# Off-by-one softmax attention and a mish MLP on one core: five tiles transposed wholly by DMA, copies, loads and outputs put in another order

## The chip, the core and the metric

One core of a Trainium2 chip runs the whole kernel. Its engines work side by side: TensorE (PE: matmuls, with the weight loads as PEld), VectorE (DVE), ScalarE (ACT), GpSimd (POOL) and SyncE (SP, which here only issues DMAs). Each runs its own list of instructions in order, and they wait for one another through semaphores. Data moves between HBM and the on-chip memory (SBUF) by DMA. In this kernel SP's queue carries all loads of q, k and v, all DMA transposes and nearly all stores; POOL's queue carries the weights. Matmul results land in PSUM, in banks of 512 fp32 numbers per partition.

The metric is the device time of one execution, in microseconds. The profile covers one execution; its times count from the start of its span.

## The reference

```python
# q, k, v: (8, 12, 448, 64) float32; moe_w_in: (768, 2048); moe_w_out: (2048, 768)
scores = matmul(q, k^T) / sqrt(64)
m = max(scores, axis=-1)
e = exp(scores - m)
attn = e / (sum(e, axis=-1) + exp(-m) + 1e-09)
x = matmul(attn, v), heads put side by side           # (3584, 768)
h = x @ moe_w_in
out = (h * tanh(softplus(h))) @ moe_w_out             # mish, then the second matmul
```

## The kernel before

*Pairs, units, stages.* The 12 heads of a batch are taken two at a time: 48 pairs, 6 in a batch. Three pairs make a unit. The first six pairs (0 to 5, the head) run by themselves in the loop at L663; from pair 6 on, the loop at L698 takes one unit after the other: unit 2 is pairs 6 to 8, unit 3 pairs 9 to 11, unit 4 pairs 12 to 14 and so on. In each unit the attention of its three pairs (12 steps) runs beside work of earlier pairs, and then comes half a batch of the first MLP matmul with its mish (the loop at L795). From unit 4 on, the second MLP matmul of earlier batches is spread over the 12 steps as filler for TensorE. Units 2 and 3 have no such filler. The head has matmuls on a constant (`keep_busy`, L287) in its place.

*One pair.* q, k and v come as fp32 (`load_pair`, L133) and are cast to bf16, mostly by POOL (`cast`, L177). q and k are transposed, by TensorE into PSUM (`transpose_pair`, L207) for pairs up to 17 and by DMA (`turn_by_dma`, L197) from 18 on. `evac_qk` (L238) copies the transposed q, scaled, and k to SBUF: one of VectorE, ScalarE or POOL. In the head, ScalarE takes both copies of the even pairs (`act=True`, L674; pair 1 too, L667) and VectorE those of the odd ones.

A pair has four steps of scores (`scores`, L309), each into one of three PSUM tiles `sc` of two banks. The fourth step fills one bank only. VectorE takes the negated row maximum (L350), ScalarE the exp with the row sum (`exps`, L355, L366), into the tile `en`. `scores_ahead` (L302) keeps three steps in flight, so a unit's first four scores are issued at its very start.

*The transposed probabilities.* `normalise` (L428) divides where that is done early and starts the DMA transpose of `en` into `eT` (L440): four chunks of 112 keys, seven blocks of 128x128 each. For pairs 0 to 4 the DMA takes three chunks, and TensorE the fourth (`turn_on_pe`, L445, with seven transposes and a copy by VectorE, L455). For pairs 5, 6 and 7 (`BY_PE`, L640) TensorE turns all of it. There are three `eT` buffers, so the transposes of pairs 3 and 4 wait until the outputs of pairs 0 and 1 have read theirs.

*The outputs.* `av_pair` (L463) multiplies `eT` by v, eight matmuls, three pairs later, and a copy takes the result into `xT`, input of the MLP. In the head and at the end the result goes to a bank of its own. In units 2 and 3 it goes into the second bank of a pair's fourth score tile, which is free (`half`, L469). From unit 4 on `scores` itself calls it, ahead of the fourth step's score, into that same bank (L323). A unit's first pair of outputs needs the `eT` that the unit before issued last among its work; for unit 5 that is pair 12.

*The weights.* `load_w` (L165) issues the next n of 20 pieces on POOL's queue: 12 of `moe_w_in`, 8 of `moe_w_out`. With `behind`, POOL first copies two elements of a pair's `eT`, so that it waits for that transpose to land. Before: 6 behind pair 4 (L687), 2 in unit 2 (L645), 5 behind pair 8 (L799), 3 in unit 3, 4 behind pair 10 (L801).

*The loads.* SP issues in the order of the program, and each load waits for a buffer (three of each kind). In units 2 to 4, steps 0, 3 and 6 (`LOAD_AT`, L636) load q and k of the pair four ahead and v of the next, and cast what came before (L735 to L740).

Of the kernel before, what the change touches and what calls it, by code (L numbers as in the profile page):

```python
# [15 lines left out]
UNIT_PAIRS = 3  # L16
# [3 lines left out]
def kernel(  # L20
# [288 lines left out]
    def scores(idx):  # L309
# [13 lines left out]
        if s == STEPS - 1 and p in av_with:  # L323
            av_pair(av_with.pop(p), bank=sc[:, 1, :], beside=idx)
# [28 lines left out]
        st["sc", s] = (sc, cols)  # L353

# [73 lines left out]
    def normalise(p, dma=True):  # L428
        st = att[p]
        en = st["en"]  # L430
        for i in range(NTILE if divided(p) else 0):
            nc.vector.tensor_scalar(  # L432
                out=en[:, :, i, 0:SP_], in0=en[:, :, i, 0:SP_],
                scalar1=st["rden"][:, i : i + 1], scalar2=None, op0=ALU.mult,
            )
        eT = eT_pool.tile([128, NT, 2 * S], BF16, tag="eT", name="eT")
        st["eT"] = eT
        if dma:
            n = NT - 1 if p < HEAD else NT
            nc.sync.dma_start_transpose(  # L440
                out=eT[:, 0:n, :].rearrange("c j (i q) -> c (j i) q", q=128),
                in_=en[:, 0:n].rearrange("q j i c -> q (j i c)"),
            )
# [19 lines left out]
    def av_pair(p, bank=None, beside=None, half=None, hold=False):  # L463
# [5 lines left out]
        if half is not None:  # L469
            bank = free_half(half)  # L470
            mms = av_beside.setdefault(half * STEPS + STEPS - 1, [])
        av = mo_take() if bank is None else bank
# [17 lines left out]
        def evac():  # L490
            to = xT[b][:, hp, :]
            if divided(p):
                read = (nc.scalar.copy if p in BY_PE else nc.vector.tensor_copy)(out=to, in_=av[:, 0:S])  # L493
# [4 lines left out]
            if half in half_exp:  # L498
                apart(read, half_exp[half])
            elif beside is not None or half is not None:  # L500
                av_read[beside if half is None else half * STEPS + STEPS - 1] = read
            if bank is None:
# [142 lines left out]
    W_AT = ({5: 2}, {1: 3})  # L645
# [17 lines left out]
    for p in range(HEAD):  # L663
        for s in range(STEPS):
# [8 lines left out]
            if s == 2:  # L673
                evac_qk(p + 2, act=p % 2 == 0)  # L674
# [5 lines left out]
            if s == 1 and p:  # L680
                turn_on_pe(p - 1, NT - 1)
            if s == 2:
# [3 lines left out]
                if p == HEAD - 1:  # L686
                    load_w(6, behind=p - 1)  # L687
# [10 lines left out]
    for u in range(UNITS_PER_B, N_UNITS + 2 * UNITS_PER_B):  # L698
# [11 lines left out]
        for n in range(steps):  # L710
# [24 lines left out]
            if n in LOAD_AT and u <= first_mm2:  # L735
                at = p0 + LOAD_AT.index(n)
                load_pair(at + LEAD, "qk")
                load_pair(at + 1, "v")
                cast(at + LEAD - 1, "qk")
                cast(at, "v")  # L740
# [54 lines left out]
        for f in range(FF_U):  # L795
            if moe:
                mm1_mish(b, w * FF_U + f)
            if u == UNITS_PER_B and f == 3:
                load_w(5, behind=p0 + 2)  # L799
# [52 lines left out]
```

## Time and profile before

| | us |
|---|---|
| median of three runs | 466.2 (465.72 to 466.34) |
| the profiled execution | 465.11 |
| its span, first to last instruction | 463.3 |
| TensorE busy | 441.6 (95%) |
| VectorE busy | 347.3 (75%) |
| ScalarE busy | 331.9 (72%) |
| POOL busy | 184.6 (40%) |

The median of the runs is 1.1 us above the profiled execution, and that one is 1.8 above its span. The granted TensorE clock was 0.991 on average, and full except in the first 20 us and the last.

A row of the timeline gives start, length, engine (SPq and POOLq are the queues' own), line, operation, output and inputs, the count of merged instructions, and in brackets how long the engine idled before and what ended that. A row of groups gives the busy time and mean ns of one after the bar, then the idle time before the group. A row by stage gives the stretch, its length, the busy time of each engine with instruction counts, the granted clock, the DMA share (the 16 engines' mean busy share; it passes 1 where packets of two queues overlap) and GB/s. In what follows "tile p" is the `eT` of pair p.

### The profile page before, as it was taken

How to read it: one execution, taken by the hardware profiler on the slowest of the kernel's cores; microseconds unless marked ns; L12 is line 12 of the kernel's file. 1: busy time of each engine (PE TensorE's matmuls, PEld its weight loads, DVE VectorE, ACT ScalarE, POOL GpSimd, SP SyncE). 2: the span in 40 equal slices, each digit the busy share in tenths (PEclk: the TensorE clock that was granted, in tenths of full speed). 3: DMA queues.
4: the chain of work that ended last, by engine and by line, in shares of the span. 5: the costliest groups of instructions: out<-in, count | busy, mean ns of one | idle time of the engine just before them, and what ended most of it. 6: DMA issues, size and time to landing. Idle time of an engine off the chain costs nothing.

```text
span 463.3 us, 8712 instructions
## 1 busy us (share of the span) xinstructions
PE 441.6 (95%) x2975; PEld 242.8 (52%) x2975; DVE 347.3 (75%) x674; ACT 331.9 (72%) x876; POOL 184.6 (40%) x267
## 2 busy tenths in 40 slices
PE   6878998999999999999999999999999999999996
PEld 3334555445555555555555555555555554556563
DVE  5899879688798998989898979889888969311021
ACT  4999888798797878787887978787878778221300
POOL 4434629043256271736464643727363610100000
PEclk8899999999999999999999999999999999999999
DMA  8999999999999999999999999999999492911122
GB/s 237 252 209 234 223 225 208 220 233 248 234 268 268 230 253 215 293 223 269 235 270 244 270 219 242 255 234 241 260 271 238 118 253 59 253 48 35 34 69 68
DMA packets 232492, 97.93 MB, mean 211 GB/s; under 512 B 189312, under 2 KB 228992, under 8 KB 232448
## 3 DMA queue, kind: packets, MB, share of 16 engines
q1 hardware_dynamic: 224928, 91.06, 83.0%
q0 software_dynamic: 7488, 6.29, 8.7%
q8 instruction: 23, 0.38, 0.3%
q14 instruction: 21, 0.17, 0.1%
q10 hardware_dynamic: 32, 0.02, 0.0%
HBM read 45.61 MB, written 11.01 MB: 122 GB/s over the span
## 4 chain that ended last, share of the span: by engine, by line
PE 70%; ACT 12%; DVE 10%; DMA 4%; issue 2%; SPq 0%; DVEq 0%; ACTq 0%
PE mo L532 26%; PE mo L595 23%; ACT en L366 10%; PE sc L329 7%; DVE negm L350 7%; PE sc L480 6%; PE sc L532 4%; DMA eT<-en 2%; DMA q_f<-in_q_dram 1%; DVE xT L493 1%; DVE eT L455 1%; PE sc L335 1%; DMA k_f<-in_k_dram 1%; PE mo L480 1%; DVE o_sb L578 1%
## 5 line engine op out<-in xcount | busy, mean ns | idle before, releaser
L366 ACT ACTIVATE en<-sc,negm 128x448 bf16<-128x448 f32 x336 | 209.4, 642 | 29.5 <-DVE negm L350 27.7
L350 DVE TENSOR_REDUCE negm<-sc 128x2 f32<-128x896 f32 x192 | 180.9, 969 | 42.3 <-PE sc L329 33.1
L595 PE MATMUL mo<-w_out_sb,gT 128*128 128x384 bf16 (+1 forms) x1024 | 166.7, 306 | 0.4 <-DVE rb L420 0.4
L532 PE MATMUL mo<-xT,w_in_sb 128*128 128x448 bf16 x660 | 132.2, 352 | 1.5 <-ACT gT L548 0.9
L595 PEld LDWEIGHTS <-gT 128*128 128x128 bf16 x1024 | 96.4, 98 | 56.1 <-issue 1.9
L270 POOL TENSOR_SCALAR qd<-qT_all 64x448 bf16<-64x448 bf16 x60 | 80.1, 1335 | 85.5 <-DMA qT_all<-q_cast 65.0
L532 PEld LDWEIGHTS <-w_in_sb 128*128 128x128 bf16 x768 | 74.2, 98 | 70.4 <-issue 4.1
L548 ACT ACTIVATE gT<-mo 128x448 bf16<-128x448 f32 x110 | 58.3, 544 | 68.0 <-PE mo L532 67.9
L432 DVE TENSOR_SCALAR en<-en,rden 128x448 bf16<-128x448 bf16 x280 | 89.2, 394 | 0.6
L366 ACT ACTIVATION_READ_ACCUMULATOR en<-sc,negm 128x1 f32 x336 | 71.6, 213 | 0.0
L578 DVE COPY o_sb<-mo 128x384 f32<-128x384 f32 (+1 forms) x64 | 31.9, 498 | 50.1 <-PE mo L595 49.3
L329 PE MATMUL sc<-kT_all,qd 128*128 128x448 bf16 x252 | 67.6, 354 | 0.0
L480 PE MATMUL sc<-eT,v_bf 112*64 112x448 bf16 x336 | 39.8, 357 | 2.0 <-ACT en L366 1.1
L329 PEld LDWEIGHTS <-qd 128*128 128x128 bf16 x252 | 24.6, 98 | 28.7 <-issue 12.9
L191 POOL CAST q_cast<-q_f 112x512 bf16<-112x512 f32 x47 | 28.7, 611 | 5.2 <-DMA q_f<-in_q_dram 5.2
L480 PEld LDWEIGHTS <-v_bf 112*64 112x64 bf16 x384 | 19.9, 109 | 20.5 <-issue 12.9
L742 POOL COPY marks<-en 1x2 bf16<-1x2 bf16 x12 | 2.1, 174 | 68.6 <-DVE en L432 68.6
L191 POOL CAST k_cast<-k_f 112x512 bf16<-112x512 f32 x47 | 28.6, 609 | 0.8 <-PE sc L329 0.5
L191 POOL CAST v_bf<-v_f 112x512 bf16<-112x512 f32 x48 | 28.1, 607 | 1.7 <-DMA v_f<-in_v_dram 1.7
L532 PE MATMUL sc<-xT,w_in_sb 128*128 128x448 bf16 x108 | 23.2, 353 | 0.0
L493 DVE CAST xT<-sc 128x448 bf16<-128x448 f32 x35 | 21.5, 615 | 0.0
L548 ACT ACT_TABLE_LOAD x14 | 18.0, 1283 | 0.8 <-PE mo L532 0.2
(64 smaller groups left out, 235.3 us busy)
## 6 DMA issues: line engine op xcount, KB each, us to landing
k_f<-in_k_dram SPq DMA_DIRECT2D x48, 224.0 KB, 5.1
q_f<-in_q_dram SPq DMA_DIRECT2D x48, 224.0 KB, 4.9
v_f<-in_v_dram SPq DMA_DIRECT2D x48, 224.0 KB, 5.0
w_in_sb<-in_moe_w_in_dram POOLq DMA_DIRECT2D x12, 256.0 KB, 8.9
w_out_sb<-in_moe_w_out_dram POOLq DMA_DIRECT2D x8, 384.0 KB, 12.2
out_dram<-o_sb SPq DMA_DIRECT2D x7, 336.0 KB, 3.5
out_dram<-o_sb SPq DMA_DIRECT2D x8, 288.0 KB, 4.8
out_dram<-o_sb SPq DMA_DIRECT2D x8, 240.0 KB, 3.8
```

The costliest lines, as they stand in the source:

```text
L191: nc.gpsimd.tensor_copy(out=to[nm], in_=src)
L270: q_reads.append(by.tensor_scalar(out=qd[rows, :, h, :], in0=q_ps[rows, 0:S].rearrange("d (i r) -> d i r", i=QB), scalar1=SCALE, scalar2=N ...
L329: nc.tensor.matmul(sc[:, bk, 0:S], lhsT=qT[:, i].rearrange("d h r -> d (h r)"), rhs=kT, start=True, stop=True,)
L350: half_max[p] = nc.vector.tensor_reduce(out=negm, in_=sc[:, 0 : len(cols), 0:S], axis=AX.X, op=ALU.max, negate=True)
L366: e = nc.scalar.activation(out=st["en"][:, :, c, 0:SP_], in_=sc[:, bk, 0:S].rearrange("q (j c) -> q j c", j=NT), func=AF.Exp, bias=st["neg ...
L432: nc.vector.tensor_scalar(out=en[:, :, i, 0:SP_], in0=en[:, :, i, 0:SP_], scalar1=st["rden"][:, i : i + 1], scalar2=None, op0=ALU.mult,)
L480: mm = nc.tensor.matmul(av[h * 64 : (h + 1) * 64, 0:S], lhsT=v_bf[:, h, j * D : (j + 1) * D], rhs=e_h, start=(j == 0), stop=(j == NT - 1),)
L493: read = (nc.scalar.copy if p in BY_PE else nc.vector.tensor_copy)(out=to, in_=av[:, 0:S])
L532: nc.tensor.matmul(bank[:, 0:S], lhsT=w_in_sb[:, dm, ff * 128 : (ff + 1) * 128], rhs=xT[b][:, dm, :], start=(dm == 0), stop=(dm == DM_T - 1),)
L548: nc.scalar.activation(out=gT[:, ff, b % 2 * S : b % 2 * S + S], in_=h_ps[:, 0:S], func=AF.Mish)
L578: nc.vector.tensor_copy(out=o_sb[:, cols.start : cols.start + n_dve], in_=st["o"][:, 0:n_dve])
L595: nc.tensor.matmul(st["o"][:, 0:n_cols], lhsT=gT[:, ff, i * 128 : (i + 1) * 128], rhs=w_out_sb[:, ff, cols], start=(ff == 0), stop=(ff == ...
```

## The change

- Pairs 0 to 4: all four chunks of `eT` by DMA. `turn_on_pe` is no longer called for them.
- In the head, VectorE makes the copies of q and k of every pair from 2 on.
- Weights: 3 pieces behind tile 3, 3 behind tile 4, none in the steps of unit 2, 7 behind tile 8; the other seven as before.
- Loads: v of pair 8 comes first in unit 2; v of 7, q and k of 12 and v of 9 move from the steps of unit 2 into its MLP loop, behind the transpose of tile 8. The cast of v of 7 moves to the start of unit 3.
- Outputs from unit 4 on: called behind the fourth step's score and its maximum, with the bookkeeping that units 2 and 3 use (`half`). The copy of pair 7's output moves from ScalarE to VectorE; pair 6's stays.

```diff
@@ scores
-        if s == STEPS - 1 and p in av_with:
-            av_pair(av_with.pop(p), bank=sc[:, 1, :], beside=idx)
...
         st["sc", s] = (sc, cols)
+        if s == STEPS - 1 and p in av_with:
+            av_pair(av_with.pop(p), half=p)
@@ normalise
-            n = NT - 1 if p < HEAD else NT
             nc.sync.dma_start_transpose(
-                out=eT[:, 0:n, :].rearrange("c j (i q) -> c (j i) q", q=128),
-                in_=en[:, 0:n].rearrange("q j i c -> q (j i c)"),
+                out=eT.rearrange("c j (i q) -> c (j i) q", q=128),
+                in_=en.rearrange("q j i c -> q (j i c)"),
             )
@@ av_pair
-        av = mo_take() if bank is None else bank
+        av = mo_take() if half is None else free_half(half)
...
-                read = (nc.scalar.copy if p in BY_PE else nc.vector.tensor_copy)(out=to, in_=av[:, 0:S])
+                by_act = p == HP
+                read = (nc.scalar.copy if by_act else nc.vector.tensor_copy)(out=to, in_=av[:, 0:S])
+                if by_act:
+                    apart(read, half_max[half])
@@ head loop
-                evac_qk(p + 2, act=p % 2 == 0)
+                evac_qk(p + 2)
...
-            if s == 1 and p:
-                turn_on_pe(p - 1, NT - 1)
...
-                if p == HEAD - 1:
-                    load_w(6, behind=p - 1)
+                if p >= HEAD - 2:
+                    load_w(3, behind=p - 1)
@@ weights in steps
-    W_AT = ({5: 2}, {1: 3})
+    W_AT = ({}, {1: 3})
@@ unit loop, steps
-                load_pair(at + LEAD, "qk")
-                load_pair(at + 1, "v")
+                if u > UNITS_PER_B or n < LOAD_AT[-1]:
+                    load_pair(at + LEAD, "qk")
+                if u > UNITS_PER_B:
+                    load_pair(at + 1, "v")
+                elif n == 0:
+                    load_pair(at + 2, "v")
+                if u == UNITS_PER_B + 1 and n == 0:
+                    cast(at - 2, "v")
                 cast(at + LEAD - 1, "qk")
-                cast(at, "v")
+                if u > UNITS_PER_B or n != LOAD_AT[1]:
+                    cast(at, "v")
@@ unit loop, MLP
+            if u == UNITS_PER_B and f == 2:
+                load_pair(p0 + 1, "v")
+                load_pair(nxt + UNIT_PAIRS, "qk")
+                load_pair(nxt, "v")
             if u == UNITS_PER_B and f == 3:
-                load_w(5, behind=p0 + 2)
+                load_w(7, behind=p0 + 2)
```

9 lines of the change are left out of this document (4 added, 5 removed).

## The prediction

> **What bounds the kernel now.** I read the page's shares, then the busy time by stage, then the chain of waits, then the timeline of the queues. Stages (start:end, then length and busy time of each engine, granted clock, DMA share):
>
> ```profile
> core 0: us, PE busy (x) PEld busy (x) DVE busy (x) ACT busy (x) POOL busy (x), PEclk, DMA share, GB/s
> 13.77:39.43 25.66, 20.14 (x187) 10.12 (x187) 23.35 (x40) 24.88 (x83) 7.77 (x21) 0.99 1.13 223
> 92.40:118.50 26.10, 24.66 (x183) 13.81 (x181) 20.61 (x41) 21.59 (x56) 9.22 (x16) 1.00 1.13 237
> 118.50:144.26 25.76, 25.39 (x158) 13.84 (x157) 23.42 (x49) 20.38 (x53) 12.03 (x14) 1.00 1.11 259
> 144.26:169.60 25.34, 25.24 (x159) 13.89 (x158) 22.13 (x43) 20.27 (x53) 13.18 (x16) 1.00 1.05 243
> ```
>
> Three regimes stand here. In the head (pairs 1 to 5) ScalarE is busy 24.88 of 25.66 us, VectorE 23.35; TensorE waits for them, and part of its 20.14 is filler. In the units behind it TensorE is busy 25.24 of 25.34 us. And everywhere the DMA share is over 1: the 16 engines always have something queued. Between head and steady state the chain goes through that queue. The chain's piece, and TensorE's row at its end:
>
> ```profile
> 112.32 10.99 DMA eT<-en
> ```
> ```profile
> 123.44 0.95 PE L480 MATMUL sc<-eT,v_bf 112*64 112x448 bf16 x8 [0.37 <-DMA eT<-en]
> ```
>
> The page's median from issue to landing, for the same transfer:
>
> ```profile
> eT<-en SPq DMA_TRANSPOSE x45, 5.4
> ```
>
> The first tile of the unit that ends at 118 (pair 12) takes 10.99 us where 5.4 is usual, as it stands in its queue behind loads and shares the engines with weights; TensorE then waits 0.37 us. So at 123.3 TensorE and DMA arrive together. Whatever the head gains passes into the total only if that tile also lands earlier.
>
> **The change part by part.** *Transposes.* Five tiles go from 21 blocks of 128x128 to 28; 35 transposes on TensorE and five VectorE copies vanish. SP's queue (start, time to issue):
>
> ```profile
> 13.98 3.68 SPq L440 DMA_TRANSPOSE eT<-en  x1
> ...
> 25.99 3.65 SPq L440 DMA_TRANSPOSE eT<-en  x1
> ...
> 30.35 0.41 SPq L140 DMA_DIRECT2D k_f<-in_k_dram  x1
> 31.52 3.28 SPq L440 DMA_TRANSPOSE eT<-en  x1
> ...
> 35.52 0.41 SPq L140 DMA_DIRECT2D k_f<-in_k_dram  x1
> 37.30 3.28 SPq L440 DMA_TRANSPOSE eT<-en  x1
> ...
> 57.85 5.71 SPq L440 DMA_TRANSPOSE eT<-en  x1
> ...
> 85.56 11.38 SPq L440 DMA_TRANSPOSE eT<-en  x3
> ...
> 112.32 15.61 SPq L440 DMA_TRANSPOSE eT<-en  x3
> ```
>
> Three full tiles in an emptied queue take 11.38, that is 3.79 each; tiles of three chunks 3.28. Marginal cost 0.5 a tile, 2.5 us for five. Bounds: by blocks 3.79 x 7/28 = 0.95 a tile, 4.7 us; from below 0.14 (3.79 against 3.65), 0.7 us. I take 2.5, as the 3.28 rows are the ones with an undisturbed issue. Against it stands queue time that is free now: SP has nothing to issue from 30.76 to 31.52 and from 35.93 to 37.30 (2.1 us), since tiles 3 and 4 wait for a buffer that the outputs of pairs 0 and 1 release, and these come earlier when the head is faster.
>
> By the Trainium skill (VectorE: DVE Perf Modes, "The three transpose paths" and "Rules for kernel authors"), a 128x128 transpose costs 390 ns on TensorE and 1309 ns by DMA, with TensorE recommended; 35 moved blocks would then add 45.8 us of DMA time against 13.7 saved. The rows above disagree: a full tile of 28 blocks is issued in 3.79 us. By them the rule's warning shrinks to the range given.
>
> *ScalarE and VectorE in the head.* Groups of that stage (count, busy us, mean ns), then ScalarE's and VectorE's timeline:
>
> ```profile
> L455 DVE COPY eT<-mo 112x896 bf16<-112x896 bf16 x4 | 2.5, 615 | 0.0
> ...
> L261 ACT ACTIVATE qd<-mo 128x448 bf16<-128x448 bf16 x2 | 1.1, 554 | 0.0
> L280 ACT COPY kT_all<-mo 128x448 bf16<-128x448 bf16 x2 | 1.1, 552 | 0.0
> ```
> ```profile
> 13.77 0.28 ACT L379 ACTIVATE expm<-negm 128x7 f32<-128x7 f32 x1
> ...
> 20.28 0.63 ACT L366 ACTIVATE en<-sc,negm 128x448 bf16<-128x448 f32 x1 [0.60 <-DVE negm L350]
> ...
> 22.73 0.55 ACT L261 ACTIVATE qd<-mo 128x448 bf16<-128x448 bf16 x1
> ...
> 23.57 0.68 ACT L366 ACTIVATE en<-sc,negm 128x448 bf16<-128x448 f32 x1
> ...
> 39.43 0.22 ACT L379 ACTIVATE expm<-negm 128x7 f32<-128x7 f32 x1
> ```
> ```profile
> 18.04 0.61 DVE L455 COPY eT<-mo 112x896 bf16<-112x896 bf16 x1
> 18.57 0.38 DVE L263 TENSOR_SCALAR qd<-mo 128x448 bf16<-128x448 bf16 x1
> ...
> 19.17 2.61 DVE L350 TENSOR_REDUCE negm<-sc 128x2 f32<-128x896 f32 x3
> ```
>
> The two ScalarE copies hold the chain of exps from 22.73 to 23.57, 0.84 us. They leave for pairs 2, 4 and 6: 2.5 us of the engine that sets this stage. VectorE takes the same two for 0.60 (18.57 to 19.17), 1.8 us in all, and loses five copies of 0.53 (18.04 to 18.57), 2.7 us; so it carries 0.9 less, but in every pair now, close to ScalarE's load. I take 2.0 us off the head; bounds 0 (VectorE's reductions end last instead) and 3.0 (ScalarE's 0.60 us of waiting at 20.28, where one pair has the transposed copy and the q and k copies on VectorE, goes too). The TensorE transposes sat beside filler, and cost nothing before or after.
>
> *Weights and loads.* POOL's queue:
>
> ```profile
> 42.71 0.17 POOL L169 COPY marks<-eT 1x2 bf16<-1x2 bf16 x1 [2.42 <-DMA eT<-en]
> 42.83 4.54 POOL L174 DMA_DIRECT2D w_in_sb<-in_moe_w_in_dram  x6
> ...
> 51.16 1.46 POOL L174 DMA_DIRECT2D w_in_sb<-in_moe_w_in_dram  x2
> ...
> 67.20 0.17 POOL L169 COPY marks<-eT 1x2 bf16<-1x2 bf16 x1 [8.20 <-DMA eT<-en]
> ```
>
> Three pieces leave some 6 us sooner, behind tile 3 (31.52 + 5.4 = 36.9, against 42.71); two pieces (51.16) and four loads go behind tile 8, whose 5.71 us of issue (57.85) shows a full queue in front of it. The number of pieces and loads ahead of tile 12 stays the same, so these edits only reorder work of a queue that is never empty: 0. The new mark makes POOL wait, with the scale factors and the casts of pair 8 queued behind it; those are used only in the next unit. Cover gone, the three issues (4.54 / 2 = 2.3 us) would show. From the other side: if the queue runs dry in front of tile 8 because four loads now stand behind it, the dry time is lost, up to the 5.71 - 3.79 = 1.9 us that the backlog cost there.
>
> *Outputs behind scores.* Steady units, TensorE, VectorE, ScalarE:
>
> ```profile
> 152.91 0.81 PE L595 MATMUL mo<-w_out_sb,gT 128*128 128x384 bf16 x4
> 153.67 0.95 PE L480 MATMUL sc<-eT,v_bf 112*64 112x448 bf16 x8
> ...
> 157.84 0.66 PE L595 MATMUL mo<-w_out_sb,gT 128*128 128x192 bf16 x6
> 158.60 0.95 PE L480 MATMUL sc<-eT,v_bf 112*64 112x448 bf16 x8
> ```
> ```profile
> 150.09 0.62 DVE L350 TENSOR_REDUCE negm<-sc 128x1 f32<-128x448 f32 x1 [1.27 <-PE sc L329]
> ```
> ```profile
> 150.75 0.63 ACT L366 ACTIVATE en<-sc,negm 128x448 bf16<-128x448 f32 x1 [0.63 <-DVE negm L350]
> ```
>
> Today the fourth score of a pair stands behind eight output matmuls (0.95 us); VectorE idles 1.27 and ScalarE 0.63 for it. Swapped, both get it 0.9 us sooner. TensorE itself loses little to it: normally the outputs start 0.05 us before the previous row's modelled end (153.67 against 153.72), in every second unit 0.10 behind it (158.60 against 158.50), so 0.15 us a unit pair; six pairs give 0.9 us. Bounds 0 (the same wait moves to the score) and 1.8 (twice that). Waiting outputs no longer hold a score. The moved copy of pair 7's output costs VectorE one such row,
>
> ```profile
> L493 DVE CAST xT<-sc 128x448 bf16<-128x448 f32 x35 | 21.5, 615 | 0.0
> ```
>
> 0.6 us, in a stretch whose end waits for DMA anyway.
>
> **Sum.** Tile 12's landing: +2.5 (blocks) - 2.1 (queue time now unused) - 0.7 (the first tile is issued at 13.98, right behind pair 0's last exps at 13.77, and one 0.84 leaves before that; most of it counts) = -0.3. The head's 2.0 does not pass beyond this, and turns into a longer wait at tile 12. Steady units: -0.9. Together -1.2 us. The profiled execution took 465.11 (span 463.3 and 1.8 around it), so 463.9; the three runs' median is 466.2, 1.1 above it, so 465.0. Bounds: landing -2.8 (2.1 and 1.4 of an earlier start against 0.7) to +4.7, steady 0 to -1.8.
>
> **The rivals.**
> - *The gain passes whole.* If tile 12 is no longer late, the total keeps the head's 2.0 and the units' 0.9: 463.3; with the head at 3.0, 462.3. For it: the first three tiles show that loads behind them keep the engines full, so a seventh more blocks may fit. Against: DMA shares of 1.13 in both stages.
> - *The extra blocks are paid in full (slower).* Blocks cost 0.95 a tile, nothing is absorbed, tile 12 lands 4.7 us later, at 128.0, and TensorE waits there. With 0.9 back from the units that is +3.8: 470.0. It decides as soon as the landing slips by more than 0.9. For it: tile 12's 10.99 us, and 15.61 for its three tiles against 11.38. Against: 3.28 for three chunks and 3.79 for four.
> - *The head isn't shortened.* VectorE's copies in each pair delay its reductions by the 0.60 that ScalarE gets back, and tiles are issued no earlier: +2.5 at the landing, -0.9: 467.8.
> - The Trainium skill (DMA: Bandwidth & Descriptors, "Queues, rings and completion order") says that each DMA engine takes turns between queues packet by packet, so weights issued earlier would slow tile 4 and speed nothing; that is the second rival's mechanism, and no row of this profile separates it.
>
> **How the numbers follow.** Forecast 0.40 (own range 463.5 to 466.5), gain whole 0.10, paid in full or most of it 0.30, head not shortened 0.20. Within 0.2% (0.93 us, about what a measurement of this kernel can tell from no change) lie a quarter of the forecast's chance (0.10) and, where the third rival is half absorbed, 0.10 of it: same 0.20. Faster 0.30 + 0.10 = 0.40. Slower 0.40. The range takes the head's 3.0 at the low end and all blocks paid at the high end, each cut a little: 462.5 to 469.5.
>
> **What would show it.** Right: ScalarE's two copies gone from the head and the expm row of pair 5 near 37.4 instead of 39.43; full tiles there issued in about 3.8 us; tile 12 landing near 123 and a TensorE wait in front of its outputs of about 2 us instead of 0.37; units of about 25.2 us. Wrong: tile 12 landing at 125 or later (blocks paid), no wait for it at all (gain passes), POOL or TensorE waiting for weights or for casts of pairs 8 and 12, or a VectorE busier than 95% of the head. The forecast falls if any unit behind 120 grows longer than 25.34.

## The result, and the profile after

The kernel after takes 472.94 us (median of six runs, 472.2 to 475.0), the kernel before 465.99 beside it (465.68 to 467.78). The ratio is 1.0146, 95% interval 1.0119 to 1.0173: 7 us slower, outside the range of the prediction and on its other side. Here and below, medians are over all runs and ratios over the undisturbed ones alone, so that the two can differ by some tenths of a per cent.

The profiled execution of after is the slowest of its six (475.0, span 473.2, mean granted clock 0.978), so its trace holds 9.9 us more than that of before, not 7. Where they arise is read off the row in which ScalarE loads its table for the mish of each MLP, one row a unit:

| start of the MLP of | before | after | difference |
|---|---|---|---|
| unit 2 | 57.84 | 59.37 | +1.5 |
| unit 3 | 85.56 | 85.57 | 0.0 |
| unit 4 | 109.88 | 116.11 | +6.2 |
| unit 5 | 136.68 | 146.33 | +9.7 |
| the last | 389.89 | 400.15 | +10.3 |

So nearly all of it (9.7 of 10.3 us) is lost before 147 us, in units 2, 4 and 5, and unit 3 wins 1.5 back. The busy time by stage of after, with the columns as before:

```profile
12.22:37.29 25.07, 21.10 (x166) 8.97 (x166) 24.11 (x43) 23.48 (x79) 8.53 (x21) 0.93 1.14 233
93.40:125.30 31.90, 26.47 (x183) 14.30 (x182) 20.99 (x42) 21.62 (x57) 9.29 (x16) 0.95 1.17 225
125.30:154.70 29.40, 27.01 (x159) 14.28 (x158) 22.95 (x50) 20.42 (x54) 13.25 (x17) 0.94 1.05 255
154.70:180.10 25.40, 25.33 (x159) 13.60 (x158) 21.73 (x43) 20.15 (x54) 13.28 (x18) 1.00 0.99 235
```

The head ends 2.1 us earlier, where 2.0 was forecast (expm of pair 5):

```profile
37.29 0.25 ACT L379 ACTIVATE expm<-negm 128x7 f32<-128x7 f32 x1
```

One pair of executions fixes this only roughly: in the traces of before, after and the kernels below this row starts at 39.4 to 41.1 us where the head is that of before (four traces, mean 40.1), and at 36.9 to 37.7 where it is that of after (six, mean 37.2). VectorE is busy 24.11 of the 25.07 us, 96%.

Units 4 and 5, which took 26.10 and 25.76 us, take 31.90 and 29.40. TensorE is idle in them for the difference between length and busy time, 5.4 and 2.4 us, and the clock of 0.95 and 0.94 makes its busy time longer too. Behind them a unit takes 25.40, where it took 25.34. SP's transposes and POOL's queue up to that point:

```profile
12.67 5.51 SPq L439 DMA_TRANSPOSE eT<-en  x1
...
19.90 6.69 SPq L439 DMA_TRANSPOSE eT<-en  x1
...
27.81 4.50 SPq L439 DMA_TRANSPOSE eT<-en  x1
...
33.54 4.05 SPq L439 DMA_TRANSPOSE eT<-en  x1
...
38.83 4.56 SPq L439 DMA_TRANSPOSE eT<-en  x1
...
59.38 3.56 SPq L439 DMA_TRANSPOSE eT<-en  x1
...
85.57 17.69 SPq L439 DMA_TRANSPOSE eT<-en  x3
```
```profile
41.30 0.18 POOL L169 COPY marks<-eT 1x2 bf16<-1x2 bf16 x1 [8.58 <-DMA eT<-en]
41.42 2.38 POOL L174 DMA_DIRECT2D w_in_sb<-in_moe_w_in_dram  x3
...
47.96 0.18 POOL L169 COPY marks<-eT 1x2 bf16<-1x2 bf16 x1 [2.55 <-DMA eT<-en]
48.08 2.17 POOL L174 DMA_DIRECT2D w_in_sb<-in_moe_w_in_dram  x3
50.25 0.21 POOL L391 CAST hl<-rden 128x7 bf16<-128x7 f32 x1
```

The five tiles of the head take 25.31 us to issue (5.51 + 6.69 + 4.50 + 4.05 + 4.56). In before they take 19.28: the four rows that the prediction shows, and tile 1, which it left out:

```profile
19.38 5.39 SPq L440 DMA_TRANSPOSE eT<-en  x1
```

That is 6.0 more for 35 blocks, 1.2 a tile, where 0.5 was taken and 0.95 was the bound. The mark rows date two landings: tile 3 at 41.3, tile 4 at 47.96, 5.2 us later than the 42.71 of before, although it was issued only 1.5 us later (38.83 against 37.30). POOL then issues three pieces, and only behind them come the scale factors of pair 5, at 50.25. In before:

```profile
47.33 0.25 POOL L391 CAST hl<-rden 128x7 bf16<-128x7 f32 x1
```
```profile
51.25 0.70 PE L411 MATMUL mo<-ident,hl 128*64 128x128 bf16 x16
```

There they were begun at 47.33 and used at 51.25, 3.9 us later. With the shorter head TensorE wants them 3 us sooner, and they come 2.9 us later. TensorE's three rows with a long wait in after, all of it new except the first 0.37 us of the last:

```profile
50.51 1.27 PE L411 MATMUL mo<-ident,hl 128*64 128x128 bf16 x16 [2.40 <-POOL hl L391]
...
101.26 1.71 PE L478 MATMUL sc<-eT,v_bf 112*64 112x448 bf16 x8 [4.85 <-DMA eT<-en]
...
131.65 1.54 PE L478 MATMUL sc<-eT,v_bf 112*64 112x448 bf16 x8 [2.39 <-DMA eT<-en]
```

They wait for the factors of pair 5, for tile 9 and for tile 12 (which landed at 131.6 instead of 123.3). What makes each worse stands in the length of the row: the same sixteen or eight matmuls take 0.70 and 0.95 us in other places, and 1.27, 1.71 and 1.54 here. Three stretches of unit 2 in after, by stage:

```profile
50.00:53.00 3.00, 2.49 (x24) 1.37 (x24) 0.00 (x0) 1.12 (x4) 2.91 (x8) 0.50 1.15 303
53.00:57.00 4.00, 4.00 (x16) 1.18 (x13) 2.54 (x3) 2.00 (x7) 1.24 (x3) 0.53 0.99 169
...
58.00:60.50 2.50, 2.50 (x19) 1.15 (x16) 2.09 (x6) 2.48 (x6) 0.48 (x3) 1.00 0.00 0
```

Behind the wait the granted clock (third column from the right) is 0.50 and stays there for some 6.8 us. And from 58.0 to 60.5 the DMA share is 0.00: the queue that "is never empty" is empty, since the loads that stood there wait behind tile 8. It was not always full in before either: between 122 and 123 us, right ahead of tile 12's landing at 123.3, the DMA share is 0.11, and in after it is 0.14 between 130 and 131, ahead of the landing at 131.6. So the last microsecond before that landing is not a wait behind other bytes; what it is, no run here shows.

### The profile page after: what moved, and what is told of

It is laid out like the page before. It is cut to its first block, busy times and chain, and to the rows that moved or that the text cites. A ratio compares the mean times of both kernels' runs of the same rounds, so it can differ in the third digit from the quotient of the medians.

```text
span 473.2 us, 8561 instructions
## 1 busy us (share of the span) xinstructions
PE 447.2 (95%) x2940; PEld 241.0 (51%) x2940; DVE 349.7 (74%) x676; ACT 328.5 (69%) x869; POOL 185.5 (39%) x268
## 4 chain that ended last, share of the span: by engine, by line
PE 78%; DMA 6%; DVE 5%; ACT 5%; issue 4%; POOL 2%; SPq 1%; DVEq 0%; POOLq 0%
PE mo L596 27%; PE mo L533 26%; PE sc L327 9%; PE sc L478 8%; PE sc L533 4%; ACT en L366 4%; DMA eT<-en 4%; DVE negm L348 4%; DMA k_f<-in_k_dram 1%; POOL w_in_sb L174 1%; PE sc L333 1%; PE sc L290 1%; PE sc L225 1%; PE mo L478 1%; SPq L140 1%
## 5 line engine op out<-in xcount | busy, mean ns | idle before, releaser
L596 PE MATMUL mo<-w_out_sb,gT 128*128 128x384 bf16 (+1 forms) x1024 | 168.4, 308 | 0.0
L596 PEld LDWEIGHTS <-gT 128*128 128x128 bf16 x1024 | 93.8, 98 | 66.9 <-issue 16.5
L270 POOL TENSOR_SCALAR qd<-qT_all 64x448 bf16<-64x448 bf16 x60 | 80.0, 1334 | 89.5 <-DMA qT_all<-q_cast 39.2
L478 PE MATMUL sc<-eT,v_bf 112*64 112x448 bf16 x336 | 41.9, 373 | 7.2 <-DMA eT<-en 7.2
L478 PEld LDWEIGHTS <-v_bf 112*64 112x64 bf16 x384 | 18.7, 111 | 32.0 <-issue 22.6
L748 POOL COPY marks<-en 1x2 bf16<-1x2 bf16 x12 | 2.1, 176 | 67.4 <-DVE en L432 67.4
```

The lines of the kernel that those rows point to most:

```text
L270: q_reads.append(by.tensor_scalar(out=qd[rows, :, h, :], in0=q_ps[rows, 0:S].rearrange("d (i r) -> d i r", i=QB), scalar1=SCALE, scalar2=N ...
L478: mm = nc.tensor.matmul(av[h * 64 : (h + 1) * 64, 0:S], lhsT=v_bf[:, h, j * D : (j + 1) * D], rhs=e_h, start=(j == 0), stop=(j == NT - 1),)
L596: nc.tensor.matmul(st["o"][:, 0:n_cols], lhsT=gT[:, ff, i * 128 : (i + 1) * 128], rhs=w_out_sb[:, ff, cols], start=(ff == 0), stop=(ff == ...
```

## The experiments

All are variants of the kernel before or of the kernel after; each ran beside the kernel before on the same chip.

### One part of the change at a time

*Outputs behind scores, alone.*

```diff
-        if s == STEPS - 1 and p in av_with:
-            av_pair(av_with.pop(p), bank=sc[:, 1, :], beside=idx)
...
         st["sc", s] = (sc, cols)
+        if s == STEPS - 1 and p in av_with:
+            av_pair(av_with.pop(p), half=p)
```

> The kernel before with one edit: from unit 4 on the outputs stand behind the fourth score. Queue theory (the loss is made by the DMA queue: tiles 9 and 12 land late): nothing is changed in the queue, so 466.0 within 0.8 us, units of the steady state 25.3 to 25.4 us. Order theory (outputs behind scores hold up TensorE): most of the 7 us, 470 or more. The prediction on record had 0.9 us of gain for this edit, 465.1.

466.84 us, ratio 1.0012 (0.9984 to 1.0041): nothing that can be measured. The wait is not removed; it has another name. In its trace the second pair of a unit now holds ScalarE up:

```profile
154.37 0.64 ACT L366 ACTIVATE en<-sc,negm 128x448 bf16<-128x448 f32 x1 [1.51 <-DVE negm L348]
```

With a wait of 0.40 later in this unit that makes 1.91 us; in the same unit of before ScalarE waited 0.63, 0.81 and 0.51, or 1.95.

*Five tiles wholly by DMA, alone.*

```diff
-            n = NT - 1 if p < HEAD else NT
+            n = NT
...
-            if s == 1 and p:
-                turn_on_pe(p - 1, NT - 1)
```

> The kernel before with one edit: pairs 0 to 4 turned wholly by DMA, no fourth chunk on TensorE. Queue theory: seven blocks cost 0.7 to 0.95 us of queue time a tile, 3.5 to 4.7 us, and tile 12 lands near 127 in place of 123.3: 468.5 to 471. Prediction on record: 0.5 us a tile, and no more than 466.8. Rival (the queue had room; the loss is in the moved weights and loads): 466 within 0.8.

472.18 us (four runs), ratio 1.0119 (1.0087 to 1.0152): 5.5 us, most of the loss. POOL, then TensorE, in its trace:

```profile
46.93 0.18 POOL L169 COPY marks<-eT 1x2 bf16<-1x2 bf16 x1 [7.86 <-DMA eT<-en]
47.05 4.52 POOL L174 DMA_DIRECT2D w_in_sb<-in_moe_w_in_dram  x6
51.57 0.21 POOL L391 CAST hl<-rden 128x7 bf16<-128x7 f32 x1
```
```profile
51.83 0.93 PE L411 MATMUL mo<-ident,hl 128*64 128x128 bf16 x16 [2.03 <-POOL hl L391]
...
55.00 0.93 PE L532 MATMUL mo<-xT,w_in_sb 128*128 128x448 bf16 x2 [0.87 <-DMA w_in_sb<-in_moe_w_in_dram]
...
57.26 0.93 PE L532 MATMUL mo<-xT,w_in_sb 128*128 128x448 bf16 x2 [1.33 <-DMA w_in_sb<-in_moe_w_in_dram]
```

Tile 4 lands 4.2 us later than in before, and everything that hangs behind it is late at once: the factors (2.03 us of waiting), then the first weights (0.87 and 1.33). Unit 2's MLP begins at 62.5 instead of 57.8, and these 4.7 us stay, the larger part of the 6.9 at the last MLP (396.8 against 389.9). A wait of 1.65 us for tile 15 in unit 6 adds most of the rest. There is no wait at tile 12 in this one: the price is paid in unit 2, not where the prediction looked.

*VectorE's copies of q and k, alone.*

```diff
-                evac_qk(p + 2, act=p % 2 == 0)
+                evac_qk(p + 2)
```

> The kernel before with one edit: VectorE makes the q and k copies of all pairs from 2 on in the head, and keeps the five copies of the fourth chunk. Queue theory: whatever the head gains or loses up to 2 us is swallowed at tile 12, 465.5 to 466.5. Rival (VectorE's load in the head is what costs): pair 5's last exps later than 39.4 and 467.5 or more.

465.40 us, ratio 0.9984 (0.9955 to 1.0014): no change. The head itself is not shorter. Its expm of pair 5 starts at 39.92, within the 39.4 to 41.1 us of the unchanged head, and VectorE is now the busiest engine of that stage (here in the stretch of before's):

```profile
13.77:39.43 25.66, 21.10 (x184) 10.12 (x183) 24.69 (x46) 23.07 (x75) 8.27 (x22) 0.94 1.09 231
```

24.69 of 25.66 us, and 26.36 of 27.50, 96%, in this kernel's own stage (12.42 to 39.92). Where three or all five of the PSUM copies of the fourth chunks go as well, this row stands at 36.9 to 38.1; where they go and ScalarE keeps its copies of q and k, at 39.2 and 38.6. The head's gain takes both edits.

*The kernel after, fourth chunk back on TensorE.*

```diff
-                out=eT.rearrange("c j (i q) -> c (j i) q", q=128),
-                in_=en.rearrange("q j i c -> q (j i c)"),
+                out=eT[:, 0 : (NT - 1 if p < HEAD else NT), :].rearrange("c j (i q) -> c (j i) q", q=128),
+                in_=en[:, 0 : (NT - 1 if p < HEAD else NT)].rearrange("q j i c -> q (j i c)"),
...
+            if s == 1 and p:
+                turn_on_pe(p - 1, NT - 1)
```

> The changed kernel with one part undone: the fourth chunk of pairs 0 to 4 on TensorE again, with VectorE's copy. Queue theory: the queue loses 3.5 to 4.7 us of blocks, tiles 9 and 12 land that much sooner than in the changed kernel, and POOL's wait for tile 4 shrinks: 467.5 to 469.5. Rival (the reordered weights and loads, or the order of outputs, make the loss): 472 or more, as the changed kernel.

470.15 us, ratio 1.0072 (1.0047 to 1.0097): still 3.4 us slower than before, with not one block more on the DMA queue. The outputs and the copies of q and k cost nothing alone, nor does pair 7's copy (below), so this is left for the reorder of weights and loads. The two prices, 5.5 and 3.4, add up to more than the 7 us of the whole change; they are in part the same lateness. How the reorder costs, its queues tell (SP, POOL, TensorE), though the profiled execution is far the slowest of its eight (475.57 us, the next 471.15), so that its waits are longer than usual:

```profile
36.86 9.17 SPq L439 DMA_TRANSPOSE eT<-en  x1
```
```profile
35.59 2.40 POOL L174 DMA_DIRECT2D w_in_sb<-in_moe_w_in_dram  x3
...
51.94 0.17 POOL L169 COPY marks<-eT 1x2 bf16<-1x2 bf16 x1 [12.09 <-DMA eT<-en]
```
```profile
54.50 0.93 PE L411 MATMUL mo<-ident,hl 128*64 128x128 bf16 x16 [3.62 <-POOL hl L391]
```

Tile 4, of three chunks as in before, is issued 0.4 us earlier than there and lands 9.2 us later, at 51.94. The three pieces of weights behind tile 3 were put on POOL's queue just ahead of it.

### What the reorder costs, and where

*Factors first on POOL.* In the kernel after:

```diff
-                if p >= HEAD - 2:
+                if p == HEAD - 2:
                     load_w(3, behind=p - 1)
...
     denominators(HEAD - 1)
+    load_w(3, behind=HEAD - 2)
```

> The kernel after, with one change: the three weights behind tile 4, and the mark that makes POOL wait for that tile, stand behind the scale factors of pair 5 in POOL's queue instead of in front of them. Theory (POOL's queue): TensorE's wait of 2.40 us for these factors at 50.51 is gone, the granted clock stays at 1.0 there (it was 0.50 from 52 to 56), unit 2's MLP starts near 55.5 instead of 59.4, and tile 8 is issued as much earlier; if that passes through, about 469. Rival (the DMA queue sets the end): tiles 9 and 12 land when they did (101.3, 131.6), TensorE waits the longer for them, and the time stays within 1 us of 472.9.

469.95 us, ratio 1.0065 (1.0034 to 1.0096): 3.0 us back. The wait for factors is gone, the clock is 1.00 through unit 2, whose MLP begins at 55.6, as the theory had it. Tile 9 still lands late, and TensorE waits there as long as in after (4.90 us, with the clock at 0.50 behind it), since it arrives sooner. The wait at tile 12 has gone. The number lies between the two theories: a part passes, a part turns into waiting.

*Loads back.* In the kernel after, the four loads return to unit 2's steps:

```diff
-                if u > UNITS_PER_B or n < LOAD_AT[-1]:
-                    load_pair(at + LEAD, "qk")
...
+                load_pair(at + LEAD, "qk")
+                load_pair(at + 1, "v")
                 cast(at + LEAD - 1, "qk")
-                if u > UNITS_PER_B or n != LOAD_AT[1]:
-                    cast(at, "v")
+                cast(at, "v")
...
-            if u == UNITS_PER_B and f == 2:
-                load_pair(p0 + 1, "v")
-                load_pair(nxt + UNIT_PAIRS, "qk")
-                load_pair(nxt, "v")
```

> The kernel after, with the four loads back in unit 2's steps (weights as after). Theory (the queue ran dry): the DMA share of 0.14 between 56 and 60 goes up to about 1, the loads no longer stand in front of tiles 11, 9 and 10, tile 9 lands some 2.7 us sooner than 101.3, and so does tile 12: about 470.5. Rival (order of the queue is free): tile 8 lands later by what the loads take, and the total stays within 1 us of 472.9.

470.16 us, ratio 1.0067 (1.0034 to 1.0099): 2.8 us back. The waits at tiles 9 and 12 are 1.81 and 1.86 us instead of 4.85 and 2.39. Tile 9 lands 12.7 us behind the first issue of its three tiles instead of 15.7 (101.67 from 89.02, 101.26 from 85.57), so an empty queue in front of tile 8 is paid for with a fuller one in front of tiles 11, 9 and 10. By the clock it lands no sooner: the 2.7 us of the theory are not in this trace, and its wait is shorter because TensorE comes 3.5 us later. In this execution, the slowest of its ten, tile 3 landed 2.4 us earlier than in after, so its weights had longer beside tile 4, which landed at 51.80; TensorE waited 6.61 us for the factors. Its last MLP still starts 1.7 us before that of after, although it waits 4.2 us longer in unit 2.

*Six pieces behind tile 4 again.* In the kernel after:

```diff
-                if p >= HEAD - 2:
-                    load_w(3, behind=p - 1)
+                if p == HEAD - 1:
+                    load_w(6, behind=p - 1)
```

> The kernel after, with the six first weights behind tile 4 as before instead of three behind tile 3 and three behind tile 4. Theory (weights in flight slow a transpose): tile 4, which took 9.1 us from issue (38.83) to landing, lands about 3 us sooner, near 45; POOL then issues six pieces (4.5 us), so the factors of pair 5 are ready near 49.6 and TensorE's wait in unit 2 is about 1.7 instead of 2.4; TensorE also waits for the weights themselves; total 472 to 473. Rival (28 blocks alone make tile 4 late): tile 4 lands near 47.9 all the same, the factors come at 52.6, and the total is about 475.

473.08 us, ratio 1.0128 (1.0065 to 1.019): as slow as after. But tile 4 lands sooner:

```profile
45.75 0.18 POOL L169 COPY marks<-eT 1x2 bf16<-1x2 bf16 x1 [7.69 <-DMA eT<-en]
```

It is issued at 39.11, so it takes 6.6 us against the 9.1 of after, with the same 28 blocks. What it wins POOL gives back with six issues in place of three (the factors come at 50.38).

*All weights and loads as before* (the five tiles, VectorE's copies and the outputs behind scores stay): the two diffs above for loads and for six pieces, and

```diff
-    W_AT = ({}, {1: 3})
+    W_AT = ({5: 2}, {1: 3})
...
-                load_w(7, behind=p0 + 2)
+                load_w(5, behind=p0 + 2)
```

> The kernel after, with all weights and loads where they were before; five tiles wholly by DMA, VectorE's copies and the outputs behind scores stay. Theory: the reorder costs what the queue's dry time and tile 4's company cost, so this one is faster than after; the head is 2 us shorter than in the kernel with the five tiles alone (472.2), so about 470. Rival (the head's gain turns into waiting): 472, as with the five tiles alone. Second rival (only the blocks cost): no faster than after, 472.9.

470.78 us, ratio 1.0084 (1.0048 to 1.012). 2.2 us faster than after (the two intervals just meet), about what the theory said. TensorE waits 3.35 us for the factors, 0.85 at tile 9 and 2.56 at tile 12.

*Both repairs together* (the diffs of the first two kernels of this part).

> The kernel after, with both repairs together: the weights behind tile 4 stand behind the scale factors of pair 5 on POOL, and the four loads are back in unit 2's steps. Theory (two separate costs, a wait in unit 2 and the backlog in front of tiles 11, 9 and 10): the single repairs took 3.0 and 2.8 us off, together 5 to 6: 467 to 468, with unit 2's MLP near 55.6 and TensorE's wait for tile 9 below 3 us instead of 5.0. Rival (both repair the same lateness): about 470, the wait for tile 9 grows by what unit 2 gains.

469.39 us, ratio 1.0058 (1.0032 to 1.0083). The rival: the two repairs don't add. Unit 2's MLP begins at 54.9, the earliest of all kernels, and the wait at tile 9 is 4.16 us.

*The five tiles alone, with the factors first* (the six pieces behind tile 4 go behind `denominators(HEAD - 1)` in the kernel before).

> The kernel before, with the five tiles wholly by DMA and, on POOL, the weights behind tile 4 issued behind the scale factors of pair 5. With the five tiles alone the time was 472.2. Theory (most of that edit's price is the wait on POOL's queue and the halved clock behind it): TensorE's wait of 2.0 us for the factors is gone, but the six pieces of weights still come behind a tile 4 that lands 4 us late, so it waits for them (up to 2 us), and the time is 469 to 470. Rival (the blocks' own time in the DMA queue): tiles 8, 9 and 12 land late anyway and it stays at 472.

472.78 us, ratio 1.0078 (1.0035 to 1.0121); the interval overlaps that of the five tiles alone, so the times do not tell them apart. The trace does: the wait for the factors is gone, and one for the weights has taken its place, which was the lesser part of the theory and is here the whole:

```profile
54.93 0.93 PE L532 MATMUL mo<-xT,w_in_sb 128*128 128x448 bf16 x2 [3.93 <-DMA w_in_sb<-in_moe_w_in_dram]
57.17 0.93 PE L532 MATMUL mo<-xT,w_in_sb 128*128 128x448 bf16 x2 [1.32 <-DMA w_in_sb<-in_moe_w_in_dram]
```

### Fewer blocks, and the weights between them

*Tiles 0 to 2 wholly by DMA*, in the kernel before, with VectorE's copies and the factors first:

```diff
-            n = NT - 1 if p < HEAD else NT
+            n = NT - 1 if 2 < p < HEAD else NT
...
-                evac_qk(p + 2, act=p % 2 == 0)
+                evac_qk(p + 2)
...
-            if s == 1 and p:
+            if s == 1 and p > 3:
                 turn_on_pe(p - 1, NT - 1)
...
-                if p == HEAD - 1:
-                    load_w(6, behind=p - 1)
...
     denominators(HEAD - 1)
+    load_w(6, behind=HEAD - 2)
```

> The kernel before, with q and k copied by VectorE, only tiles 0 to 2 wholly by DMA (tiles 3 and 4 keep their fourth chunk on TensorE), and the weights behind tile 4 issued behind the scale factors of pair 5. Theory (the early tiles find room, the choke is tile 4 and POOL behind it): tile 4 lands before 45, TensorE does not wait in unit 2, the head is 1 us shorter, tile 12 lands within 1 us of 123.3: 465 to 466, no slower than before. Rival (each block moved is paid in the DMA queue, wherever it stands): 21 blocks, 3 us, 469.

467.23 us, ratio 1.0013 (0.9989 to 1.0037): as fast as before. Tile 4 lands before 45, and there is no wait for factors:

```profile
44.55 0.17 POOL L169 COPY marks<-eT 1x2 bf16<-1x2 bf16 x1 [2.49 <-DMA eT<-en]
```

But TensorE, early now, waits 2.14 and 0.79 us for the first weights. Twenty-one more blocks do not cost the 3 us of the rival, and bring nothing either.

*The same with two pieces behind tile 3 and four behind tile 4.*

> As the kernel with tiles 0 to 2 wholly by DMA, VectorE's copies and the scale factors first (467.2), but the first two pieces of weights go behind tile 3 and four behind tile 4, instead of six behind tile 4. Theory (TensorE's waits for weights at 50.5 and 53.2, 3.3 us with the halved clock behind them, are what that kernel still lost): the first matmuls of the MLP find their pieces, unit 2's MLP starts near 56 instead of 59.5, and the time is 464 to 465.5, faster than before. Rival (what is put ahead of tile 4 delays it by as much): tile 4 lands 2 us later than 44.5, the other four pieces too, TensorE waits for these or for tile 4, and the time is 467 or more.

466.51 us, ratio 0.9997 (0.997 to 1.0024). Tile 4 in POOL's queue:

```profile
39.15 0.18 POOL L169 COPY marks<-eT 1x2 bf16<-1x2 bf16 x1 [0.52 <-DMA eT<-en]
39.27 1.67 POOL L174 DMA_DIRECT2D w_in_sb<-in_moe_w_in_dram  x2
...
49.93 0.18 POOL L169 COPY marks<-eT 1x2 bf16<-1x2 bf16 x1 [7.27 <-DMA eT<-en]
```

The rival, and more than it said: beside two pieces tile 4 lands 5.4 us later (49.93 against 44.55), not 2. This execution is the slowest of its twelve; in the two kernels below with the same two pieces tile 4 lands at 47.5 and 48.4. Put together, the time of tile 4 from issue to landing (its mark on POOL), one execution of each kernel:

| blocks | pieces of weights beside tile 4 | kernels | us |
|---|---|---|---|
| 21 | none | before and six others | 4.7 to 7.3 |
| 28 | none | five tiles alone; the same with factors first; after with six behind tile 4; after with weights and loads as before | 7.9; 9.1; 6.6; 6.7 |
| 21 | two, issued 1.0 us behind it | tiles 0 to 2, two pieces early (three kernels) | 9.9, 9.9, 11.6 |
| 28 | three, 2.6 us behind it | after; both repairs | 9.1; 9.1 |
| 28 | three, 1.0 us behind it | factors first; loads back | 11.7; 13.8 |
| 21 | three, 1.3 us ahead of it | after, fourth chunk on TensorE | 15.1 |

Without weights seven more blocks cost about 2 us there (medians 5.2 and 7.3; the ranges overlap). Weights beside it cost the more the earlier they are issued: next to nothing to 2.5 us for three pieces 2.6 us behind it, some 8 to 10 for three ahead of it. At the 233 GB/s that the head moves, two pieces of 256 KB are about 2.2 us and three 3.4. The three longest times, 15.1, 13.8 and 11.6, come from executions that were the slowest of their kernels, so their size is less sure than their order.

### The copy of pair 7's output

Unit 3 is 17.7 us long in after and in all its variants, and 19.8 in before. One edit had not been run alone, the copy that goes from ScalarE to VectorE. In the kernel before:

```diff
-                read = (nc.scalar.copy if p in BY_PE else nc.vector.tensor_copy)(out=to, in_=av[:, 0:S])
+                by_act = p == HP
+                read = (nc.scalar.copy if by_act else nc.vector.tensor_copy)(out=to, in_=av[:, 0:S])
+                if by_act:
+                    apart(read, half_max[half])
```

> The kernel before, with one part of the change that was not run alone yet: the copy of pair 7's output goes from ScalarE to VectorE, pair 6's stays. In the profiles of all kernels that have this edit together with VectorE's copies of q and k, unit 3 is 17.7 us long instead of 19.8, and neither the copies of q and k alone nor the outputs behind scores alone do that. Theory (it is this copy: on ScalarE it holds the exps, and TensorE waits 1.32 us for a score's buffer and 0.91 us at the start of the MLP): unit 3 is 17.7 us here too, tile 9 (used at 95.88 in before) is then wanted near 93.8 and lands soon enough, and the time is 464 to 465. Rival (the transposes are the bound there: tile 9 landed at 94.9 in before): the 2.1 us turn into waiting for tiles 9 and 12, and the time stays within 1 us of 466.

466.00 us, ratio 1.0006 (0.9987 to 1.0025). Unit 3 is 17.7 us long (67.4 to 85.1): it is this copy. In before ScalarE ended two of TensorE's waits there:

```profile
78.67 0.35 PE L335 MATMUL sc<-kT_all,qd 64*128 64x448 bf16 x1 [1.32 <-ACT en L366]
...
87.44 2.43 PE L532 MATMUL mo<-xT,w_in_sb 128*128 128x448 bf16 x12 [0.91 <-ACT gT L548]
```

The first is 0.89 here, and the second is gone. And, going by the time, the gain does not reach the end. TensorE at tile 12:

```profile
124.42 0.95 PE L480 MATMUL sc<-eT,v_bf 112*64 112x448 bf16 x8 [1.60 <-DMA eT<-en]
```

Tile 12 now keeps TensorE waiting 1.60 us instead of 0.37. That would be 1.2 of the 2.1, but one execution can't place it: the wait is 1.86 in the kernel with the outputs alone, whose queue and unit 3 are those of before, and unit 2 was 1.6 us later in this execution than in that of before, for no reason in the edit.

*The same copy in the two kernels with tiles 0 to 2 by DMA* (two pieces early; six behind tile 4).

> The kernel with tiles 0 to 2 wholly by DMA, VectorE's copies, the scale factors first and two pieces of weights behind tile 3 (466.5), with pair 7's copy moved from ScalarE to VectorE. Theory: unit 3 is 2.1 us shorter and some of that stays: 464.5 to 466. Rival: the DMA queue sets the end of units 4 and 5, TensorE waits the 2.1 us at tiles 9 and 12: 466.5.

466.27 us, ratio 1.0011 (0.9986 to 1.0037); TensorE waits 3.19 us for tile 9.

> The kernel with tiles 0 to 2 wholly by DMA, VectorE's copies and the scale factors first, six pieces behind tile 4 (467.2), with pair 7's copy moved from ScalarE to VectorE. Theory: 465 to 466.5, unit 3 shorter by 2.1 us. Rival: waits at tiles 9 and 12 take it back, 467.2.

468.13 us, ratio 1.0052 (1.0033 to 1.0071): slower than before, by half a per cent. TensorE waits 2.01 and 1.77 us for weights and 1.55 for tile 12. Unit 3 is 17.7 us in both, and nothing of it reaches the end, as the rivals said; of the waits that they named, the first has that at tile 9 and the second that at tile 12.

*Four loads behind tile 12's transposes instead of in front of them*, with pair 7's copy:

```diff
-            if n == steps - 1 and u >= first_mm2:
+            if n == steps - 1 and u > first_mm2:
                 for i in range(1, UNIT_PAIRS):
                     load_pair(nxt + UNIT_PAIRS + i, "kq")
...
                     normalise(p, dma=p not in BY_PE)
+                    if u == first_mm2 and p == p0:
+                        for i in range(1, UNIT_PAIRS):
+                            load_pair(nxt + UNIT_PAIRS + i, "kq")
```

> The kernel before with pair 7's copy moved to VectorE (466.0; unit 3 shorter by 2.1 us, and TensorE then waits 1.60 us for tile 12), and the four loads of q and k of pairs 19 and 20 issued behind tile 12's transposes instead of in front of them. Theory (tile 12's place in SP's queue sets the end): four loads of 224 KB at some 230 GB/s are 3.9 us, so tile 12 lands before it is wanted, the wait of 1.60 is gone and the time is 464 to 465, faster than before. Rival (the loads are late next, for the casts and DMA transposes of pairs 18 to 20): unit 5 or 6 gets longer by as much, 466.

466.41 us, ratio 0.9986 (0.996 to 1.0012). The wait at tile 12 is gone, as the theory said, and the time is not shorter. TensorE in unit 4:

```profile
96.82 0.97 PE L480 MATMUL sc<-eT,v_bf 112*64 112x448 bf16 x8 [2.37 <-ACT en L366]
```

ScalarE is named, but in before the same matmuls start 1.5 us behind the unit's first exp, and here 3.9; it is tile 9, which landed at 96.7. The edit can't have made this wait: the four loads are issued at 104 us or later in both orders. With the same program up to there, tile 9 landed at 94.9 in the kernel without it, which had no wait at that place. So single executions differ by about as much as is to be explained, and where the 1.60 us went isn't shown.

> The kernel with tiles 0 to 2 wholly by DMA, VectorE's copies, the scale factors first, two pieces of weights behind tile 3 and pair 7's copy on VectorE (466.3; TensorE waits 3.19 us for tile 9), with the same four loads issued behind tile 12's transposes. Theory: its wait is at tile 9, not at tile 12, so this changes it by less than 1 us: 465.5 to 466.5. Rival (anything taken out of the queue helps): 464.5.

467.39 us, ratio 1.0004 (0.9978 to 1.003), with 4.47 us of waiting at tile 9 and none at tile 12: no gain from this order, as the theory said. None of the seventeen kernels is measurably faster than before.

## Why the prediction was wrong

*What held.* The head: -2.0 forecast, -2.1 measured in these two executions, and -2.9 between the means of the traces with either head. That such a gain doesn't pass into the total: every kernel with a shorter head or a shorter unit 3 shows waits behind it, at tiles 9 and 12 or, where weights and factors come late, in unit 2. The second rival, the extra blocks paid in full, was the nearest, but 470.0 is too little, its price has no term for the weights, and its place, tile 12, is not where the five tiles alone wait.

*The step that failed first: "Marginal cost 0.5 a tile, 2.5 us for five", bounds 0.7 to 4.7.* It measured 1.2 a tile and 6.0 in all (6.5 with the five tiles alone). Its rows, 3.28 against 3.79, were issue times: three full tiles in an emptied queue against tiles 3 and 4, which had a pause in front of them; the row of tile 1, 5.39 us for three chunks, was left out. A row's length says how long SP was held, not how long the transfer took (tile 3 in after: 4.05 us held, landed 7.8 us behind its start); the landing of tile 4 (42.71 before) was the quantity that mattered, and it moved by 4.2 us in the kernel with the blocks alone.

*The step that failed with it: "these edits only reorder work of a queue that is never empty: 0".* The kernel with the fourth chunk back on TensorE prices the rest of the change at +3.4. Three things were behind it. First, the weights on POOL's queue share the engines with SP's transposes: tile 4 takes 9.1 to 15.1 us beside them, and 4.7 to 9.1 without. Second, the cover for the factors: "used only in the next unit" was right, but that unit starts at once, with 3.9 us to spare. The 2.3 us named as the price with the cover gone are close to the measured wait of 2.40 by chance: here tile 4 came 5.2 us later, three issues fewer stood behind it (2.4 us), TensorE came 3 us sooner, and the 3.9 covered the larger part. Nor has the sum a term for the halved clock behind a wait. Third, the dry queue: at most 1.9 us were named, and 2.5 us at a DMA share of 0.00 were found; taking the loads back won 2.8.

By the Trainium skill (DMA: Bandwidth & Descriptors, "Queues, rings and completion order") each engine goes round the queues packet by packet; the prediction had this as a rival that no row separated. The table of tile 4 bears on it: the traces agree that weights on another queue delay a transpose, and, where they come early, mostly by more than their own bytes take; taking turns alone does not explain that.

*The place.* The prediction looked for the end of the chain at tile 12, and put the wait there at 2 us. It is 2.39, but not for the reason given: the tile lands 8.3 us later and TensorE comes 6.2 us later. Tile 4 and tile 9 stand in the same queue ahead of it, and each had its own consumer: POOL's mark, with factors and weights behind it, and unit 4's first outputs. That a gain "turns into a longer wait" was followed for one tile out of three.

*"Steady units: -0.9"* fell: 25.40 a unit against 25.34, and the outputs alone are worth nothing measurable. It was the lower bound, the same wait moved to the score. TensorE had at most 0.10 us a unit to win there (busy 25.24 of 25.34), since it set that stage.

*"The moved copy of pair 7's output costs VectorE one such row"* had the wrong sign and the right end. It makes unit 3 2.1 us shorter, as ScalarE was what TensorE waited for there, and the gain does not reach the end. In after this hid a part of the loss: unit 2 alone loses 3.7 us (2.1 won in the head, 1.5 late at its MLP).

*What is not settled.* Why weights delay the transposes by more than their own transfer time was not tried; nor why the engines stand nearly idle right ahead of tile 12's landing; nor whether a smaller number of bytes ahead of tile 9 (fewer loads, weights later still) would let the head's and unit 3's gains through. The waits are read from one execution of each kernel, and equal programs differ in them by 1 to 2 us.

## What to carry to other kernels

Cost a DMA by its landing and by what waits for that landing, not by the time its issue took; and list every consumer, those on other engines' queues too, such as a mark that makes a queue wait. Where DMA and a compute engine arrive together at several places in a row, a shorter compute stage can turn into waiting at the next of them. Before a wait of 1 or 2 us is put down to an edit, ask whether the edit stands ahead of it at all, and how far it differs between executions of the same program. Weights put "early" on another queue are not free: they run beside whatever is urgent.

## What the runs showed of the hardware

After a wait of about 2 us or more the granted TensorE clock is halved. In after it was 0.50 behind waits of 2.40 us (unit 2, for some 6.8 us), 4.85 us (tile 9, 3.4 us) and 2.39 us (tile 12, 3.4 us), so by estimate a wait of 2.4 us costs 1.7 to 3.4 more, half the time at half the clock. The same holds for all twenty waits from 2.01 to 6.61 us (these three among them) that TensorE has behind the head in the nineteen traces. Waits of 1.42 to 1.81 us left the clock at 1.00 (six of them; one of 1.77 more comes half a microsecond behind one of 2.01); of two of 1.86 us one left it (outputs alone) and one did not (loads back: 0.66 between 130 and 135 us). By the Trainium skill (TensorE: Matmul & The Clock Gate, "Part 1: The HAM clock gate") the array falls to half its clock after an idle window of about 3.4 us, and returns to full after a busy one of that length. The half, and stretches of 3.4 us and twice that, agree with the trace of after; waits clearly shorter than that window halved the clock here.

Transposes and weights together also move less: between 44 and 48 us the kernel after with the fourth chunk on TensorE shows

```profile
44.00:48.00 4.00, 3.53 (x44) 2.24 (x44) 3.75 (x6) 3.00 (x10) 0.00 (x0) 1.00 1.37 90
```

a DMA share of 1.37 at 90 GB/s, where the stages of before have 1.1 at 220 to 260. For single microseconds that happens without weights as well: 2.15 at 132 GB/s between 121 and 122 us of before, and there all of it is SP's queue, so the share passes 1 with one queue alone. Busy engines are no measure of bytes moved.
